# Fused attention and two feed-forward layers on one core: the cosine from one sine with a quarter turn, six of eight unit pairs by seven block products, and two parts of a product in plain float32

## The chip, the cores and the metric

The kernel runs on one core of one Trainium2 chip. The time is the device time of one execution in microseconds (us); the kernel before took 519.95 us as the median of three runs. Everything below about the kernel before comes from one profiled execution of it.

## The reference, cut to what matters

```python
# q, k, v: (2, 12, 448, 64); x: (896, 768); w_in: (768, 2048); w_out: (2048, 768)
scores = cap * tanh(q @ k.T / 8 / cap)
x = softmax(scores) @ v            # heads side by side: 896 tokens x 768
h = x @ moe_w_in
x = (h * cos(h)) @ moe_w_out       # first feed-forward layer
h = x @ moe2_w_in
out = (h / (1 + exp(-h))) @ moe2_w_out
```

Everything is float32 in and out. TensorE multiplies here mostly in the format float32r: a float32 number is split into a high part, rounded to float32r, and a low part, the rest, and a product of two matrices is made of three matmuls (high by high, high by low, low by high). A matmul in plain float32 needs no split and no third product, but it goes over the moving matrix more than once: the trace lists it as two matmul instructions.

## The kernel before, in words

The attention (lines 167 to 413) goes through 12 pairs of heads in an order written out by hand. Everything after it is planned: the functions `gemm_in`, `gemm_out`, `gemm_sums` and `gemm_last` only make a list of tasks, each with an engine, a cost in ns, the values that it reads and writes, and a due time; `run_plan` (L512) then goes through that list in a simulated time, gives each engine that is free the ready task with the earliest deadline for which buffers are left, and issues the instructions in the order so found. The order on each engine is thus fixed when the kernel is built. Deadlines are worked back from TensorE's tasks (`pe`, L485), which are due at the sum of the costs of the matmuls ahead of them. The costs of the others are the linear formulas in `act` (L471, ScalarE), `dve` (L474, VectorE) and `dma` (L466).

The four matrix products are these. All of them are cut in two by two blocks, and most are done with seven block products in place of eight (Winograd's form of Strassen's method), for which sums of blocks must be formed first and sums of results afterwards.

- `gemm_in` (L896), first layer's input product. The 2048 columns are handled as 8 pairs `p` of two blocks of 128 columns. For the first `PLAIN` = 3 pairs (L99) every block is multiplied as it stands (`one_side`, `half_prods`): 2 blocks by 2 halves of the tokens by 6 slices by 3 float32r matmuls, 72 of them. For the others (`m1` to `m7`, `ORDER1` at L615) there are seven block products of 9 matmuls (`block_prod`, L884), 63 of them. A plain pair needs two weight blocks, each brought to float32 (`convert`, L649: two instructions on ScalarE, one on VectorE, the join at L663) and split (`split`, L669: the high part is a copy on ScalarE, L625, the low part a subtraction on VectorE, L628 or, negated, L631). A pair by seven products needs the same two conversions, four sums of half blocks (`ADDS`, `sums`), which the list `S1E` puts on VectorE or on accumulating DMAs of the POOL queue, the splits of the four weight operands (`A`, `S31`, `S24`, and `A22` of half the size), three copies out of PSUM on ScalarE (`m1`, `m5_`, `m6`) and two additions on VectorE (`m7`, `m3`).
- `unit` (L933) makes h cos(h) from a finished 128x448 block of h in PSUM, 32 times. It writes round(h / 2 pi) as an integer (ScalarE, L938), subtracts it from h / 2 pi (VectorE, L939), takes the sine of pi times that (ScalarE, L941), squares it (ScalarE, L942) and multiplies (sine squared - 1/2) by h (VectorE, L943), which is -1/2 h cos(h).
- `gemm_out` (L755), first layer's output product: seven products (`product`, L729) of 4 parts `q`. A part is three PSUM banks by 6 float32r matmuls, after a split of its weights (`split_w`, 768 columns) and of its activations (`split_g`, 896 columns). The tuple `WHOLE` (L622) names the parts done in plain float32 without a split: parts 0, 1 and 2 of the first product, each three banks by 2 matmuls. Split activations lie in tiles of the stock `dbl`: five, of which two are given to the raw weights (L1210, L1212), so at most three groups of activations are split ahead. Sums of activations are made by `sum_g` (list `GE`), sums of weights by `w_sum` (list `WE`), on VectorE or by accumulating DMAs.
- `gemm_sums` (L1029): second layer's input product, all 8 pairs by seven products; `S3E` places the sums of half blocks, `silu` (L1041) applies the activation.
- `gemm_last` (L1121): second layer's output product, seven products of four parts. Its 16 weight blocks are converted beforehand, by the due times in `DUE` (L605), stored to DRAM and fetched again; `LE` places the sums of weights.

The matmuls of all four stages are issued at one line, L684 (`mms`). VectorE's two-operand instructions are mostly at L628 (`sub_`), ScalarE's copies at L625 (`copy`).

Of the kernel before, what the change touches and what calls it, by code (L numbers as in the profile page):

```python
# [28 lines left out]
F32 = mybir.dt.float32  # L29
F32R = mybir.dt.float32r  # L30
I32 = mybir.dt.int32
U32 = mybir.dt.uint32
U8 = mybir.dt.uint8
AF = mybir.ActivationFunctionType
ALU = mybir.AluOpType
# [3 lines left out]
def tile_attention_ffn_ffn(  # L39
# [10 lines left out]
    nc = tc.nc  # L50
    B, H, S, D = shape
    DM = out.shape[0]
    DFF = w_in1.shape[0] * 128
    P = 128
# [15 lines left out]

    capt = const.tile([P, 1], F32, name="capt")
    scap = const.tile([P, 1], F32, name="scap")

    def get_scap(cap):
        nc.vector.tensor_copy(capt, cap)
# [20 lines left out]
    xt = [[Part(f"x{j}_{b}") for b in range(B)] for j in range(KD)]  # L96

    KMAX = KD
    PLAIN = 3  # L99
    FIRST_IN = [b * HP + n for n in range(HP) for b in range(2)]  # L100
    wjobs = []
    for w_in, w_out in ((w_in1, w_out1), (w_in2, w_out2)):
# [66 lines left out]
    with ExitStack() as actx:  # L169
# [19 lines left out]
        def v_init():  # L189
            nc.gpsimd.memset(ones[:, :2 * Q], 1.0)  # L190
            nc.gpsimd.memset(ones[:, 2 * Q:], 0.0)

# [243 lines left out]
            self.after, self.next, self.vals = set(), [], []  # L438

    tasks = []  # L440
    LAT = {"X": 0, "PE": 280, "SP": 3500, "POOL": 400, "ACT": 210, "DVE": 170}
    stock = {"ring": room, "bank": [], "half": halves, "dbl": doubles, "one": [], "raw": []}

    def do(eng, cost, fn, r=(), w=(), due=1e9, moves=0, lag=0, extra=()):
# [18 lines left out]
        tasks.append(t)  # L463
        return t

    def dma(eng, kb, fn, r, w, adds=False, **k):  # L466
        rate = 0.16 if adds else 0.38 if kb > 450 else 0.24
        cost = 350 if eng == "SP" else 900 if adds else 600
        do(eng, cost, fn, r, w, moves=kb * 1.024 / rate, lag=1700 if eng == "POOL" else 600, **k)

    def act(n, fn, r, w, **k):  # L471
        do("ACT", 1.03 * (14 + 0.963 * n), fn, r, w, **k)

    def dve(n, fn, r, w, one=False, **k):  # L474
        do("DVE", 1.03 * (95 + (0.521 if one else 1.0417) * n), fn, r, w, **k)

    def plus(eng, kb, o, a, b, r, w):
        if eng == "DMA":
# [33 lines left out]
    def run_plan(free_at):  # L512
        from heapq import heappop, heappush
        for t in tasks:
            for p in t.after:
                p.next.append(t)
        for t in reversed(tasks):
            t.dl = min([t.due] + [s.dl - t.cost - t.lat for s in t.next])
        vals = list({id(v): v for t in tasks for v in t.vals if v.pool}.values())
        queue = {k: [] for k in stock}  # L520
        for v in vals:
            v.dl = min((t.dl, t.n) for t in v.tasks)
            v.left = len(v.tasks)
            if not v.held:
                queue[v.pool].append(v)
        for q in queue.values():
            q.sort(key=lambda v: v.dl)
        count = {k: len(s) for k, s in stock.items()}
        ready = {e: [] for e in LAT}
        busy = {e: free_at.get(e, 0) for e in LAT}  # L530
        events = [(0, -1, None)] + [(x, -1, None) for x in busy.values()]
        started, line = [], 0
        for t in tasks:
            t.wait = len(t.after)
            if t.eng == "X":
                t.start = 0
                started.append(t)
                events.append((t.cost, t.n, t))
            elif not t.wait:
                ready[t.eng].append(t)  # L540
        events.sort()
        while events:
            now = events[0][0]
            while events and events[0][0] == now:
                _, _, t = heappop(events)
                if t is None:
                    continue
                for s in t.next:
                    s.wait -= 1
                    if not s.wait:  # L550
                        ready[s.eng].append(s)
                for v in t.vals:
                    if v.pool:
                        v.left -= 1
                        if not v.left:
                            for k, n in (v.gives[1] if v.gives else [(v.pool, v.n)]):
                                count[k] += n
            for e in LAT:
                if busy[e] > now:
                    continue  # L560
                for t in sorted(ready[e], key=lambda t: (t.dl, t.n)):
                    want = [v for v in t.vals if not v.held]
                    ok = True
                    for k in {v.pool for v in want}:
                        last = max(queue[k].index(v) for v in want if v.pool == k)
                        ok = ok and sum(v.n for v in queue[k][:last + 1]) <= count[k]
                    if not ok:
                        continue
                    for v in want:
                        v.held = True  # L570
                        queue[v.pool].remove(v)
                        count[v.pool] -= v.n
                    ready[t.eng].remove(t)
                    t.start = now
                    started.append(t)
                    busy[e] = now + t.cost
                    heappush(events, (busy[e], -1, None))
                    end = busy[e] + t.lat
                    if t.moves:
                        line = max(busy[e] + 1000, line) + t.moves  # L580
                        end = line + 1000 + t.lag
                    heappush(events, (end, t.n, t))
                    break
        if len(started) < len(tasks):
            stuck = sorted((t for t in tasks if not hasattr(t, "start")), key=lambda t: t.dl)[:8]
            raise RuntimeError([(t.eng, t.dl, t.wait, t.fn.__name__, [(v.pool, v.held, v in queue.get(v.pool, ()) and queue[v.pool].index(v)) for v in t.vals]) for t in stuck] + [count])
        for v in vals:
            v.left = len(v.tasks)
        for t in sorted(started, key=lambda t: (t.start, t.n)):
            for v in t.vals:  # L590
                if v.pool and v.buf is None:
                    take_buf(v)
            if t.fn:
                t.fn()
            for v in t.vals:
                if v.pool:
                    v.left -= 1
                    if not v.left:
                        give_buf(v)

    NORMS = 6900, 9700
    GE, WE, LE = [["DVE", "DMA"][n] for n in (0, 0, 0, 1)], [["DVE", "DMA"][n] for n in (0, 0, 1, 0)], [["DVE", "DMA"][n] for n in (0, 1)]
    FE = "DVE"
    S3E = [["DVE", "DMA"][n] for n in (1, 1, 0, 0, 0, 0, 0, 0)]
    DUE = [220000, 234000, 248000, 262000, 276000, 290000, 304000, 318000, 332000, 346000, 360000, 374000, 1000000000, 1000000000, 1000000000, 1000000000]  # L605
    base_s = KF + 4 * (HK + 1)
    base_l = base_s + KF

    S1E = [["DVE", "DMA"][n] for n in (1, 0, 1, 0, 1, 1, 0, 0)]
    HALF1 = [('half', 'ring'), ('half', 'half'), ('half', 'half'), ('ring', 'ring'), ('half', 'ring'), ('half', 'ring'), ('half', 'half'), ('ring', 'ring')]  # L610
    low, high = range(KD - 2), range(KD - 2, KD)
    PLAIN_ORDER = [(0, 0), (1, 0), (2, 0), (0, 1, low), (1, 1, low), (0, 1, high), (1, 1, high), (2, 1)]
    for n in range(3, 2 * PLAIN):
# [5 lines left out]
    ORDER1.append((4, HP - 1))  # L619


    WHOLE = ((0, 1, 2), (), (), (), ())  # L622

    def copy(out, src, scale=1.0):
        nc.scalar.activation(out=out, in_=src, func=AF.Copy, scale=scale)  # L625
# [23 lines left out]
    def convert(i, out, outs, view, due=1e9, pool="raw"):  # L649
# [12 lines left out]
        def f_join():  # L662
            nc.vector.scalar_tensor_tensor(out=view(), in0=w(1), scalar=3, in1=w(0), op0=ALU.logical_shift_left, op1=ALU.bitwise_or)  # L663
        k = {"due": due}
        act(n, f_word, [], [raw], **k)
        act(n, f_scale, [], [raw], **k)
        dve(n, f_join, [raw], outs, **k)

    def split(n, hi, lo, vhi, vlo, src, r, neg=False):  # L669
        act(n, lambda: copy(vhi(), src(), -1.0 if neg else 1.0), r, [hi])  # L670
        dve(n, lambda: (neg_sub if neg else sub_)(vlo(), src(), vhi().bitcast(F32)), [hi, *r], [lo])

    def pair_of(pool="half"):
# [222 lines left out]
    def gemm_in():  # L896
# [36 lines left out]
        def unit(name, p, bank):  # L933
            t, subs = y_in(name, p // 2, gx)
            c = p % 2
            h, r = lambda: bank.buf[:, :S], lambda: t.buf[:, c, :]
            w = [subs[c]]
            act(S, lambda: copy(r().bitcast(I32), h(), 1.0 / (2.0 * math.pi)), [bank], w)  # L938
            dve(S, lambda: nc.vector.scalar_tensor_tensor(out=r(), in0=h(), scalar=1.0 / (2.0 * math.pi), in1=r().bitcast(I32),  # L939
                                                          op0=ALU.mult, op1=ALU.subtract), [bank], w)  # L940
            act(S, lambda: nc.scalar.activation(out=r(), in_=r(), func=AF.Sin, scale=math.pi), [table], w)  # L941
            act(S, lambda: nc.scalar.activation(out=r(), in_=r(), func=AF.Square), [], w)  # L942
            dve(S, lambda: nc.vector.scalar_tensor_tensor(out=r(), in0=r(), scalar=-0.5, in1=h(), op0=ALU.add, op1=ALU.mult), [bank], w, due=clock["pe"] + 5000)  # L943

        both_m = {}

# [319 lines left out]
```

## Time and profile before

| | |
|---|---|
| median of 3 runs | 519.95 us (519.59 to 520.43) |
| profiled execution | 519.64 us, of it 517.8 us from the first to the last instruction |
| TensorE busy | 99% |
| VectorE busy | 82% |
| ScalarE busy | 80% |
| granted TensorE clock | 1.000 |

Times in the profile are from the span's start. A line of a group of instructions names the source line, the engine (PE is TensorE, PEld its weight load, DVE is VectorE, ACT is ScalarE, POOL is GpSimd), the operation, what is written and read, the shapes and the number of instructions; then the busy time in us and the mean of one in ns, and the engine's idle time just before them, with the engine that ended it. The tiles are named by role: `bank` is PSUM, `v` a buffer of the planner, `hl` a tile of split weights, `x` the split attention output, `wraw` weights as loaded, `e`, `sc` and `scap` belong to the attention.

### The profile page before, as it was taken

Reading aid. Unit: us, or ns where it says so; the run is one execution under the profiler, and the core shown is the slowest. Engines: PE = TensorE matmul, PEld = TensorE weight load, DVE = VectorE, ACT = ScalarE, POOL = GpSimd, SP = SyncE. Lnnn points to the kernel's source line nnn. Section 1 sums busy time; section 2 is a strip of 40 time slices with the busy share of each in tenths; the row PEclk is TensorE's granted clock in tenths of the full one; section 3 lists DMA queues with packets and bytes.
Section 4 is the critical chain, followed back from the end, with each engine's and each line's share of the span. In section 5 each row is a group of like instructions: output and inputs, shape, how many; then the busy total and the mean of one; then the engine's idle time right before and its main releaser. Section 6 shows DMA issues by size and latency. Waiting matters only on the chain.

```text
span 517.8 us, 7246 instructions
## 1 busy us (share of the span) xinstructions
PE 510.7 (99%) x2637; PEld 420.4 (81%) x2637; DVE 424.8 (82%) x597; ACT 413.3 (80%) x583; POOL 63.3 (12%) x86
## 2 busy tenths in 40 slices
PE   8999999999999999999999999999999999999997
PEld 5444443799999997699999999999999999999996
DVE  5388997999989899999999999876779878965660
ACT  6999998699999989999777594999989664546341
POOL 0145442000210000001401111000000011400000
PEclk9999999999999999999999999999999999999999
DMA  8146464288615135799973343978798975940111
GB/s 308 59 128 192 123 206 135 78 332 238 170 31 184 61 108 197 240 330 273 196 200 84 88 104 80 375 268 299 282 346 275 381 140 105 246 92 0 54 53 54
DMA packets 27559, 92.12 MB, mean 178 GB/s; under 512 B 4536, under 2 KB 10212, under 8 KB 27524
## 3 DMA queue, kind: packets, MB, share of 16 engines
q1 hardware_dynamic: 19488, 70.89, 39.6%
q0 software_dynamic: 7680, 20.45, 18.1%
q8 instruction: 21, 0.34, 0.3%
q10 hardware_dynamic: 356, 0.32, 0.2%
q14 instruction: 14, 0.11, 0.1%
HBM read 72.75 MB, written 10.66 MB: 161 GB/s over the span
## 4 chain that ended last, share of the span: by engine, by line
PE 96%; ACT 2%; issue 1%; DVE 0%
PE bank L684 81%; PE po L273 5%; PE sc L239 4%; PE sm L291 2%; PE sc L243 2%; PE po L283 2%; ACT e L251 1%; PE warm L347 1%; ACT e L257 1%; DVE e L299 0%; DVE zero L356 0%; DVE v L1204 0%; ACT v L625 0%; PE sm L284 0%; DVE sums L318 0%
## 5 line engine op out<-in xcount | busy, mean ns | idle before, releaser
L684 PE MATMUL bank<-v,hl 128*128 128x448 f32 x1449 | 301.5, 367 | 0.0
L684 PEld LDWEIGHTS bank<-v,hl 128*128 128x128 f32 x1449 | 272.1, 188 | 25.5 <-issue 0.7
L628 DVE TENSOR_TENSOR v<-v,v 128x896 fp32r<-128x896 f32 (+4 forms) x112 | 108.7, 991 | 30.7 <-ACT v L625 30.1
L625 ACT ACTIVATE v<-v 128x896 fp32r<-128x896 f32 (+2 forms) x83 | 70.0, 853 | 56.4 <-PE bank L684 49.6
L628 DVE TENSOR_TENSOR hl<-v,hl 128x768 fp32r<-128x768 f32 (+1 forms) x89 | 79.2, 898 | 5.2 <-ACT hl L625 4.9
L625 ACT ACTIVATE hl<-v 128x768 fp32r<-128x768 f32 (+1 forms) x89 | 70.0, 797 | 1.3 <-PE bank L684 1.1
L684 PE MATMUL bank<-x,hl 128*128 128x448 f32 x288 | 59.9, 366 | 0.0
L625 ACT ACTIVATE v<-bank 128x448 f32<-128x448 f32 (+2 forms) x82 | 43.8, 541 | 18.8 <-PE bank L684 17.9
L684 PEld LDWEIGHTS bank<-x,hl 128*128 128x128 f32 x288 | 54.0, 188 | 5.0 <-DVE xs L310 0.7
L657 ACT ACTIVATE wraw<-wraw 128x768 int32<-128x768 uint8 x61 | 55.3, 917 | 2.9 <-DMA wraw<-in_moe_w_out 2.8
L660 ACT ACTIVATE wraw<-wraw 128x768 f32<-128x768 f32 x61 | 55.5, 913 | 0.0
L684 PE MATMUL bank<-v,v 128*128 128x448 f32 x225 | 54.8, 395 | 0.0
L684 PEld LDWEIGHTS bank<-v,v 128*128 128x128 f32 x225 | 42.3, 188 | 9.3 <-issue 5.9
L251 ACT ACTIVATE e<-sc,scap 128x896 f32<-128x896 f32 (+1 forms) x48 | 40.0, 911 | 6.7 <-PE sc L239 6.7
L479 POOL DMA_DIRECT2D v<-v x24 | 22.5, 936 | 167.2 <-ACT v L625 95.3
L663 DVE SCALAR_TENSOR_TENSOR v<-wraw 128x768 int32<-128x768 int32 x40 | 37.9, 952 | 5.7 <-ACT wraw L660 5.1
L257 ACT ACTIVATE e<-e,capt 128x3136 f32<-128x3136 f32 (+2 forms) x13 | 35.2, 2709 | 0.4
L273 PE MATMUL po<-e,vf 128*64 128x448 f32 x144 | 29.4, 540 | 0.4 <-ACT e L257 0.4
L273 PEld LDWEIGHTS po<-e,vf 128*64 128x64 f32 x144 | 10.2, 137 | 17.3 <-issue 16.3
L312 POOL DMA_DIRECT2D sums<-xs x22 | 17.5, 801 | 49.8 <-DVE sums L318 41.1
L628 DVE TENSOR_TENSOR v<-v 128x384 f32<-128x384 f32 (+1 forms) x42 | 23.2, 561 | 0.3
L1143 POOL DMA_DIRECT2D v<-wd x8 | 7.0, 878 | 126.6 <-DVE hl L628 102.1
(77 smaller groups left out, 460.8 us busy)
## 6 DMA issues: line engine op xcount, KB each, us to landing
wraw<-in_moe_w_out SPq DMA_DIRECT2D x32, 768.0 KB, 5.5
wraw<-in_moe_w_in SPq DMA_DIRECT2D x29, 768.0 KB, 6.6
wd<-wx SPq DMA_DIRECT2D x16, 384.0 KB, 5.4
v<-wd SPq DMA_DIRECT2D x16, 384.0 KB, 7.7
raw<-in_qkv POOLq DMA_DIRECT2D x9, 480.0 KB, 4.7
v<-v POOLq DMA_DIRECT2D x8, 384.0 KB, 7.5
v<-wd POOLq DMA_DIRECT2D x8, 384.0 KB, 6.4
rb<-rs SPq DMA_DIRECT2D x24, 112.0 KB, 3.5
```

What stands on the lines that cost most here:

```text
L239: nc.tensor.matmul(ps[:, u, :S], kk[rows, cols], qq[rows, :S], start=m == 0, stop=m == 2)
L251: nc.scalar.activation(out=e32[p][:, 2 * t:2 * t + n, :], in_=sc.pop((p, t))[:, :n, :S], func=AF.Tanh, scale=scap)
L257: nc.scalar.activation(out=e, in_=e, func=AF.Exp, scale=capt)
L273: nc.tensor.matmul(po[u * D:(u + 1) * D], vf[p][:, 2 * t + u, :], e32[p][:, 2 * t + u, :], start=first and n == 0, stop=last and n == len( ...
L312: (nc.gpsimd if p < NPT - 1 else nc.scalar).dma_start(sums[p][:, y], x[y * Q:y * Q + D + 1:D])
L479: dma("POOL", kb, lambda: nc.gpsimd.dma_start(o(), b(), accum_op=ALU.add), r, w, adds=True)
L625: nc.scalar.activation(out=out, in_=src, func=AF.Copy, scale=scale)
L628: nc.vector.tensor_tensor(out=out, in0=a, in1=b, op=op)
L657: nc.scalar.activation(out=b[:, :, 0], in_=b.bitcast(U8)[:, :, 3], func=AF.Copy, scale=1.0 / 32, bias=-0.5 + 1.0 / 64)
L660: nc.scalar.activation(out=w(1).bitcast(F32), in_=w(1).bitcast(F32), func=AF.Prelu, scale=2.0 ** -112, alpha=2.0 ** 32)
L663: nc.vector.scalar_tensor_tensor(out=view(), in0=w(1), scalar=3, in1=w(0), op0=ALU.logical_shift_left, op1=ALU.bitwise_or)
L684: nc.tensor.matmul(bank, x, y, start=first and m == 0, stop=last and m == len(ops) - 1, skip_group_check=True)
```

## The change

- `unit`: the integer is round(h / 2 pi + 1/4), the sine is taken of 2 pi times the difference plus a quarter turn, which is cos(h), and the square is left out. The quarter turn, pi / 2, is the bias of the sine instruction, read from a one-column tile `quarter` that GpSimd fills at the start. The last multiplication has the factor -1/2. The number of VectorE instructions stays.
- `PLAIN` goes from 3 to 2: pair 2 is done by seven block products. `S1E` has the sums of pair 2 on DMAs and those of pairs 3 to 7 on VectorE; before, pairs 4 and 5 had theirs on DMAs, pairs 3, 6 and 7 on VectorE.
- `WHOLE`: part 1 of the first product of `gemm_out` is split and done in float32r like the others; parts 0 and 2 stay in plain float32.
- The planner: the cost formulas of ScalarE and VectorE have other constants, with a margin of 1% where there were 3%. The high part of a split of under 800 columns becomes a task of a new kind, `COPY`: ScalarE may take it as any other, and VectorE takes it where ScalarE's queue of tasks with earlier deadlines would end less than 1000 ns ahead of the copy's deadline, or later.
- Placement: of the sums of weights in `gemm_out`, the last set is on DMAs in place of the third; in `gemm_last` both sets are on DMAs, where the first was on VectorE; in `gemm_sums` the sums of pair 2 are on DMAs. The due times of the conversions for `gemm_last` are 10 us apart in place of 14. `HALF1` exchanges the places of two pairs' split weights.

```diff
--- before.py
+++ after.py
@@ -70,6 +70,7 @@
     scap = const.tile([P, 1], F32, name="scap")
+    quarter = const.tile([P, 1], F32, name="quarter")
@@ -96,7 +97,7 @@
     KMAX = KD
-    PLAIN = 3
+    PLAIN = 2
     FIRST_IN = [b * HP + n for n in range(HP) for b in range(2)]
@@ -189,6 +190,7 @@
             nc.gpsimd.memset(ones[:, 2 * Q:], 0.0)
+            nc.gpsimd.memset(quarter, math.pi / 2.0)
@@ -438,7 +440,7 @@
     tasks = []
-    LAT = {"X": 0, "PE": 280, "SP": 3500, "POOL": 400, "ACT": 210, "DVE": 170}
+    LAT = {"X": 0, "COPY": 210, "PE": 280, "SP": 3500, "POOL": 400, "ACT": 210, "DVE": 170}
     stock = {"ring": room, "bank": [], "half": halves, "dbl": doubles, "one": [], "raw": []}
@@ -463,16 +465,19 @@
+    SPARE = 1000
+    MARGIN = 1.01
+
...
     def act(n, fn, r, w, **k):
-        do("ACT", 1.03 * (14 + 0.963 * n), fn, r, w, **k)
+        do("ACT", MARGIN * (90 + 0.84 * n), fn, r, w, **k)
     def dve(n, fn, r, w, one=False, **k):
-        do("DVE", 1.03 * (95 + (0.521 if one else 1.0417) * n), fn, r, w, **k)
+        do("DVE", MARGIN * (66 + 1.05 * n), fn, r, w, **k)
@@ -556,9 +561,12 @@
             for e in LAT:
-                if busy[e] > now:
+                if busy[e] > now or e == "COPY":
                     continue
-                for t in sorted(ready[e], key=lambda t: (t.dl, t.n)):
+                free = ready["COPY"] if e == "ACT" else []
+                if e == "DVE":
+                    free = [t for t in ready["COPY"] if max(now, busy["ACT"]) + sum(x.cost for x in ready["ACT"] + ready["COPY"] if x.dl < t.dl) > t.dl - SPARE]
+                for t in sorted(ready[e] + free, key=lambda t: (t.dl, t.n)):
                     want = [v for v in t.vals if not v.held]
@@ -571,6 +579,9 @@
                     ready[t.eng].remove(t)
+                    if t.eng == "COPY":
+                        t.eng, t.lat = e, LAT[e]
+                        t.cost = t.other if e == "DVE" else t.cost
                     t.start = now
@@ -599,15 +610,15 @@
     NORMS = 6900, 9700
-    GE, WE, LE = [["DVE", "DMA"][n] for n in (0, 0, 0, 1)], [["DVE", "DMA"][n] for n in (0, 0, 1, 0)], [["DVE", "DMA"][n] for n in (0, 1)]
+    GE, WE, LE = [["DVE", "DMA"][n] for n in (0, 0, 0, 1)], [["DVE", "DMA"][n] for n in (0, 0, 0, 1)], [["DVE", "DMA"][n] for n in (1, 1)]
     FE = "DVE"
-    S3E = [["DVE", "DMA"][n] for n in (1, 1, 0, 0, 0, 0, 0, 0)]
-    DUE = [220000, 234000, 248000, 262000, 276000, 290000, 304000, 318000, 332000, 346000, 360000, 374000, 1000000000, 1000000000, 1000000000, 1000000000]
+    S3E = [["DVE", "DMA"][n] for n in (1, 1, 1, 0, 0, 0, 0, 0)]
+    DUE = [220000, 230000, 240000, 250000, 260000, 270000, 280000, 290000, 300000, 310000, 320000, 330000, 1000000000, 1000000000, 1000000000, 1000000000]
     base_s = KF + 4 * (HK + 1)
...
-    S1E = [["DVE", "DMA"][n] for n in (1, 0, 1, 0, 1, 1, 0, 0)]
-    HALF1 = [('half', 'ring'), ('half', 'half'), ('half', 'half'), ('ring', 'ring'), ('half', 'ring'), ('half', 'ring'), ('half', 'half'), ('ring', 'ring')]
+    S1E = [["DVE", "DMA"][n] for n in (1, 0, 1, 0, 0, 0, 0, 0)]
+    HALF1 = [('half', 'ring'), ('half', 'half'), ('half', 'half'), ('half', 'ring'), ('ring', 'ring'), ('half', 'ring'), ('half', 'half'), ('ring', 'ring')]
     low, high = range(KD - 2), range(KD - 2, KD)
@@ -619,7 +630,7 @@
-    WHOLE = ((0, 1, 2), (), (), (), ())
+    WHOLE = ((0, 2), (), (), (), ())
@@ -662,12 +673,23 @@
         k = {"due": due}
-        act(n, f_word, [], [raw], **k)
-        act(n, f_scale, [], [raw], **k)
+        do("ACT", MARGIN * 800, f_word, [], [raw], **k)
+        do("ACT", MARGIN * 800, f_scale, [], [raw], **k)
         dve(n, f_join, [raw], outs, **k)
...
     def split(n, hi, lo, vhi, vlo, src, r, neg=False):
-        act(n, lambda: copy(vhi(), src(), -1.0 if neg else 1.0), r, [hi])
+        if n < 800:
+            def go():
+                if t.eng == "ACT":
+                    copy(vhi(), src(), -1.0 if neg else 1.0)
+                elif neg:
+                    nc.vector.tensor_scalar(out=vhi(), in0=src(), scalar1=-1.0, scalar2=None, op0=ALU.mult)
+                else:
+                    nc.vector.tensor_copy(vhi(), src())
+            t = do("COPY", MARGIN * (90 + 0.84 * n), go, r, [hi])
+            t.other = 100 + 0.5 * n
+        else:
+            act(n, lambda: copy(vhi(), src(), -1.0 if neg else 1.0), r, [hi])
         dve(n, lambda: (neg_sub if neg else sub_)(vlo(), src(), vhi().bitcast(F32)), [hi, *r], [lo])
@@ -935,12 +957,11 @@
             w = [subs[c]]
-            act(S, lambda: copy(r().bitcast(I32), h(), 1.0 / (2.0 * math.pi)), [bank], w)
+            act(S, lambda: nc.scalar.activation(out=r().bitcast(I32), in_=h(), func=AF.Copy, scale=1.0 / (2.0 * math.pi), bias=0.25), [bank], w)
             dve(S, lambda: nc.vector.scalar_tensor_tensor(out=r(), in0=h(), scalar=1.0 / (2.0 * math.pi), in1=r().bitcast(I32),
                                                           op0=ALU.mult, op1=ALU.subtract), [bank], w)
-            act(S, lambda: nc.scalar.activation(out=r(), in_=r(), func=AF.Sin, scale=math.pi), [table], w)
-            act(S, lambda: nc.scalar.activation(out=r(), in_=r(), func=AF.Square), [], w)
-            dve(S, lambda: nc.vector.scalar_tensor_tensor(out=r(), in0=r(), scalar=-0.5, in1=h(), op0=ALU.add, op1=ALU.mult), [bank], w, due=clock["pe"] + 5000)
+            act(S, lambda: nc.scalar.activation(out=r(), in_=r(), func=AF.Sin, scale=2.0 * math.pi, bias=quarter), [table], w)
+            dve(S, lambda: nc.vector.scalar_tensor_tensor(out=r(), in0=r(), scalar=-0.5, in1=h(), op0=ALU.mult, op1=ALU.mult), [bank], w, due=clock["pe"] + 5000)
```

## Rows read from the trace of the kernel before

**Rows 1.** Busy time, share, instructions of each engine, and the costliest group (the page).
```profile
PE 510.7 (99%) x2637; PEld 420.4 (81%) x2637; DVE 424.8 (82%) x597; ACT 413.3 (80%) x583; POOL 63.3 (12%) x86
...
L684 PE MATMUL bank<-v,hl 128*128 128x448 f32 x1449 | 301.5, 367 | 0.0
```

**Rows 2.** Chain of work that ended last, in order of time: start, length, what.
```profile
93.59 420.63 PE bank L684 x2025
...
514.63 0.39 DVE v L1204
```

**Rows 3.** Timeline of TensorE, three stretches: start, length, what, number of instructions.
```profile
99.70 4.62 PE L684 MATMUL bank<-x,hl 128*128 128x448 f32 x22
...
204.57 10.69 PE L684 MATMUL bank<-v,v 128*128 128x448 f32 x28
...
439.64 4.71 PE L684 MATMUL bank<-v,hl 128*128 128x448 f32 x22
```

**Rows 4.** Stretches: length, busy PE, PEld, DVE, ACT, POOL; granted clock, DMA share, GB/s.
```profile
91.00:123.00 32.00, 32.00 (x161) 28.12 (x158) 29.90 (x52) 27.12 (x44) 1.85 (x2) 1.00 0.65 219
123.00:160.00 37.00, 37.00 (x184) 34.27 (x183) 34.19 (x56) 36.19 (x67) 5.17 (x6) 1.00 0.53 136
160.00:200.00 40.00, 40.00 (x197) 36.72 (x196) 36.40 (x59) 37.15 (x69) 0.00 (x0) 1.00 0.36 132
200.00:218.00 18.00, 18.00 (x60) 11.05 (x59) 16.50 (x22) 17.98 (x29) 0.00 (x0) 1.00 0.54 169
218.00:260.00 42.00, 42.00 (x209) 38.93 (x208) 40.31 (x43) 38.27 (x51) 6.99 (x8) 1.00 0.96 275
260.00:310.00 50.00, 50.00 (x249) 46.34 (x248) 48.14 (x65) 37.95 (x58) 5.22 (x6) 1.00 0.48 117
...
310.00:410.00 100.00, 100.00 (x488) 91.27 (x487) 82.39 (x116) 88.79 (x138) 1.74 (x2) 1.00 0.81 285
410.00:514.00 104.00, 104.00 (x505) 94.31 (x503) 69.01 (x74) 48.80 (x65) 10.63 (x12) 1.00 0.42 101
```

**Rows 5.** Groups of instructions of ScalarE by line and shape.
```profile
L625 ACT ACTIVATE hl<-v 128x768 fp32r<-128x768 f32 x77 | 64.4, 841 | 0.2 <-DVE v L628 0.2
...
L625 ACT ACTIVATE v<-v 128x896 fp32r<-128x896 f32 x53 | 50.5, 953 | 53.5 <-PE bank L684 49.6 <-issue 3.3 <-DVE v L628 0.5
...
L625 ACT ACTIVATE v<-bank 128x448 f32<-128x448 f32 x46 | 24.9, 541 | 15.8 <-PE bank L684 15.5
L942 ACT ACTIVATE v<-v 128x448 f32<-128x448 f32 x32 | 18.3, 582 | 0.1
L941 ACT ACTIVATE v<-v 128x448 f32<-128x448 f32 x32 | 18.2, 583 | 0.8 <-DVE v L939 0.8
...
L251 ACT ACTIVATE e<-sc,scap 128x448 f32<-128x448 f32 x12 | 7.7, 639 | 0.0
```

**Rows 6.** Groups of instructions of VectorE by line and shape.
```profile
L628 DVE TENSOR_TENSOR hl<-v,hl 128x768 fp32r<-128x768 f32 x77 | 73.0, 952 | 5.0 <-ACT hl L625 4.7
L628 DVE TENSOR_TENSOR v<-v,v 128x896 fp32r<-128x896 f32 x41 | 44.7, 1090 | 26.7 <-ACT v L625 26.2
...
L628 DVE TENSOR_TENSOR v<-v 128x384 f32<-128x384 f32 x36 | 19.9, 552 | 0.3
...
L628 DVE TENSOR_TENSOR v<-bank,v 128x448 f32<-128x448 f32 x28 | 16.9, 619 | 3.1 <-PE bank L684 2.9
...
L339 DVE CAST x<-xv 128x448 fp32r<-128x448 f32 x12 | 4.7, 395 | 0.4
```

**Rows 7.** Timeline of VectorE from 218 us: neighbours, and one split.
```profile
218.91 2.09 DVE L628 TENSOR_TENSOR v<-v,v 128x896 f32<-128x896 f32 x2
...
223.76 1.09 DVE L631 SCALAR_TENSOR_TENSOR v<-v,v 128x896 fp32r<-128x896 f32 x1
```

**Rows 8.** DMA issues by what they move: number, KB each, us to landing.
```profile
v<-v POOLq DMA_DIRECT2D x8, 384.0 KB, 7.5
...
v<-v POOLq DMA_DIRECT2D x12, 192.0 KB, 3.1
```

## The prediction

> **What bounds the kernel now.** I read the page's busy times first: TensorE is busy 99% of the span [rows 1]. Busy matmuls overlap, so that alone says little; the chain of waits, in order of time, says more. From 93.59 us on it is one piece, 420.63 us of matmuls of L684, 2025 instructions, and after it only the copies and stores of the last block follow [rows 2]. In the groups these matmuls have an idle time of 0.0 [rows 1]. So after the attention the time is the number of matmuls times their pitch, and no other engine is waited for.
>
> The pitch comes from TensorE's timeline. A matmul of mean length 0.367 us [rows 1] is followed by the next after some 0.20, so the last of a stretch sticks out by 0.16. The stretch at 99.70 gives (4.62 - 0.16) / 22 = 0.2027 us, the one at 439.64 (4.71 - 0.16) / 22 = 0.2068, the plain float32 stretch at 204.57 (10.69 - 0.16) / 28 = 0.376 [rows 3]. The kernel has 3 x 72 + 5 x 63 = 531 float32r matmuls in the first input product, 25 x 18 = 450 in the first output product, 504 in each of the last two stages: 1989. The 18 plain ones appear as 36 records; 1989 + 36 are the 2025 of the chain. Check: (420.63 - 36 x 0.376) / 1989 = 0.2047, between the two pitches.
>
> Then I read the stretches, for how near the other engines are to being waited for [rows 4]. VectorE's idle time is 2.10, 2.81, 3.60, 1.50, 1.69 and 1.86 us in the six stretches from 91 to 310 us, 13.6 us in all, 11.7 of it by 260; then 17.6 and 35.0 in the last two. ScalarE has 24.3 us up to 310, 4.9 of it in the first one. The clock is granted in full (1.00, the 2.4 GHz level) in all of them.
>
> **The change on TensorE, which sets the end.** Pair 2 goes from 72 matmuls to 63: 9 x 0.2027 = 1.82 us less. The part that leaves plain float32 gives up 6 matmuls of 2 x 0.376, 4.51 us, and takes 18 of 0.2027, 3.65: 0.86 us less. Sum: 2.7 us less, with 2022 records in the chain. Nothing else in the diff adds or removes a matmul, and these counts are fixed by the code: that they don't fall is no rival.
>
> **ScalarE, off the path.** The square goes: 32 x 0.582 = 18.6 us less at most [rows 5]; the next instruction starts before the last one ends, so some 0.47 each, 15 us. The sine's bias is now a column of memory. No row shows that for a sine; the nearest is the 448-column tanh of the attention, which reads its scale from a column: 0.639 against 0.541 for a copy of the same shape out of PSUM [rows 5]. Between 0 and 0.1 us each, 0 to 3.1 in all; I take 3.1, since it is the same kind of operand. The Trainium skill, "ScalarE: Activation LUTs", section "What ACT_TABLE_LOAD costs", says that each one-column operand adds about 93 ns; by it this would be 3.0 us, and the tanh row agrees. The integer's added 1/4 is a constant in the instruction: 0, bounded by the same 0.1. Pair 2 adds three 768-column copies and a half one for two, and three copies of 0.541: 0.841 + 0.5 (half of the columns: between half of 0.841 and 0.541) + 1.6 = 3 us. The new split adds 0.841 + 0.953 = 1.8. ScalarE so loses some 7 us up to 220 us, and this covers every cost just named; without that cover, each would delay VectorE's subtraction that follows it.
>
> **VectorE, the close one.** Pair 2: three 768-column subtractions and a half one in place of two, two additions: 0.952 + 0.552 + 2 x 0.619 = 2.7 us. Sums of half blocks: 12 before, 20 after, 8 x 0.552 = 4.4. The new split: 0.952 + 1.090 = 2.0 [rows 6]. In all 9.2, or 8.2 us where neighbours overlap: two of 1.084 take 2.09 [rows 7], so 0.08 comes off for each of 13. Sums of weights in the first output product: still 12 on VectorE, but the third set, 4 x 0.87 = 3.5, falls ahead of about 260 us, where it was on DMAs. Up to 310 us VectorE must fit 8.2 us more into 2.7 us less, out of 13.6 us of idle time: 2.7 us remain. By 260 us it needs 8.2 + 3.5 + 2.7 = 14.4 out of 11.7: 2.7 us too much, unless work done ahead of need is put off. There is such work. The last of the four negated splits of the second product starts at 223.76 and ends at 224.85 [rows 7]; TensorE reaches its group after the plain stretch (to 215.1) and four groups of 18 x 0.2027, at 229.7. That is 4.9 us ahead. With three tiles for split activations it can be 11 us ahead at most. So I cost VectorE at nothing on the path: 4.9 us of lead covers 2.7 of lateness, and ScalarE's lighter load takes away some of the idle time that VectorE spends waiting for copies (26.2 us in one group over the whole kernel [rows 6], though most of it late). Copies that the planner hands to VectorE cost it 0.395 each for 448 columns [rows 6]; they are taken only where ScalarE is behind, and from 91 to 220 us it has just been relieved.
>
> **DMAs and order.** Pair 2 by seven products starts 14.6 us earlier (72 x 0.2027), after two plain pairs, 29.2 us into the stage, and its operands T1 to T4 too. Its four sums are DMAs of 192 KB, 3.1 us to landing [rows 8], for eight before in the stage, four after. In `gemm_last` a set of four 384 KB sums moves from VectorE (0.95 each) to DMAs: 0.9 us to issue on POOL as that queue's others (10.63 us for 12 [rows 4]), 7.5 to landing [rows 8], 8.4 in all, behind up to three of its own kind in the queue. A weight part is free after its split for one product and needed for the next 4 x 18 x 0.2068 = 14.9 us later; so some 6 us spare, less the splits' lead. Cost 0, bounds 0 to 3. Conversions for `gemm_last` fall 4 us each earlier, up to 44; ScalarE has 11.2 us idle from 310 to 410 [rows 4] and up to four more conversions there, of two instructions of some 0.84 each, take 7: it fits, and the short copies may go to VectorE, which has 17.6. The memset on GpSimd is ahead of the first real matmul: 0.
>
> **Sum.** The profiled execution took 519.64 us, 1.84 more than its span; 519.64 - 2.7 = 516.9. The median stands 0.31 higher: 517.3 us.
>
> **Rivals.**
> - *VectorE is the bound from about 200 to 260 us.* For it: 2.7 us remain of 13.6 in my sum, each instruction waits for something now and then, and the planner's margin falls from 3% to 1%. Against: lead, and the relief of ScalarE. It decides from the point where half of the idle time cannot be filled: then by 260 us VectorE is 2.7 + 5.9 = 8.6 us late, less 4.9 of lead, 3.7 us of waiting on TensorE, and the time is 521.0, slower than before.
> - *The pitch changes.* The two pitches of rows 3 differ by 4 ns with nothing in the code to say why; a stage of 504 matmuls that goes over is 2.0 us. The last stage at 0.2027: 515.3. A stage now at 0.2027 going to 0.2068: 519.2. Against: most of the order on TensorE stays.
> - *A sum by DMA is late*, for pair 2 or in `gemm_last`: one landing of 3.1, at 520.4. For it: the bounds above. Against: transfers have shares to spare (0.65 and 0.42 busy in these stretches [rows 4]). The Trainium skill, "SBUF — State Buffer", section "SBUF: two separate sides", holds that a copy from float32 on VectorE locks GpSimd out while it writes descriptors for such a DMA; by it each copy handed to VectorE could add its 0.4 us to a sum beside it. No row here shows a POOL issue so prolonged; with 6 us spare it would take many at once, and by rows it ends at 520.4 as well: 0.01 of this rival's chance.
>
> **How the numbers follow.** TensorE stays fed: 0.66, 516.6 to 518.0. VectorE bound: 0.14, 518.9 to 522. Pitch faster 0.06, slower 0.08. DMA late 0.06. A measurement of this kernel can tell about 0.2%, 1.0 us, from no change. Under 518.9 lie the first case, the fast pitch and a little of the rest: 0.75; within 1.0 us the slow pitch, the late DMA and mild cases of VectorE: 0.14; above 521.0 the rest of VectorE's: 0.11. The range of 515.3 to 520.4 leaves out part of VectorE's case and little of the fast pitch.
>
> **What would show it.** Right: one unbroken piece of L684 with 2022 records from 93.6 us to 511.5, no waits of PE or PEld on DVE or ACT of over 0.3 us, no group at L942, VectorE over 97% busy from 91 to 310 us, the sine about 0.1 us longer, ScalarE's idle time up to 310 us above 30. Wrong: idle time of L684 put down to DVE around 200 to 260 us, or a pitch away from 0.2027 ahead of 310 us, or from 0.2068 after 410, or waits on DMAs behind the sums at L479.

## The result, and the profile after

The changed kernel took 514.29 us in the median of 4 runs (513.87 to 514.91), the kernel before 519.86 beside it: ratio 0.9891, 95% interval 0.9873 to 0.9908. It is faster, as forecast, but by 5.6 us in place of 2.6, and 1.0 us below the low end of the range.

The page's busy times, and the chain of work that ended last (start, length, what), of the changed kernel; they answer to [rows 1, 2]:

```profile
PE 504.6 (99%) x2634; PEld 419.1 (82%) x2634; DVE 425.9 (83%) x608; ACT 404.3 (79%) x553; POOL 66.5 (13%) x91
```

```profile
93.25 415.11 PE bank L706 x2022
...
508.77 0.39 DVE v L1225
```

The matmuls are still one unbroken piece, with the 2022 records that the count gave. But it is 5.52 us shorter, where 9 + 6 x 2 records fewer and 18 more were worth 2.7. The rest is in the pitch. TensorE's timeline in the stretches of [rows 3]:

```profile
99.77 4.42 PE L706 MATMUL bank<-x,hl 128*128 128x448 f32 x21
...
207.51 4.67 PE L706 MATMUL bank<-v,v 128*128 128x448 f32 x12
...
439.67 4.62 PE L706 MATMUL bank<-v,hl 128*128 128x448 f32 x22
```

With the tail of 0.16 taken off, the first is 0.2027 us a matmul as before, the plain float32 one 0.376 as before, and the last stage (4.62 - 0.16) / 22 = 0.2027, where it was 0.2068: 504 x 4.0 ns = 2.0 us. The stage ahead of it changed too, in part: in the changed kernel its matmuls go over between the two pitches every few dozen. The busy times of the two late stages' matmuls (length, PE, PEld, then granted clock, DMA share, GB/s), of before and then of after:

```profile
310.00:405.00 95.00, 95.00 (x464) 86.68 (x463) 1.00 0.80 279
412.00:505.00 93.00, 93.00 (x452) 84.47 (x451) 1.00 0.44 102
```

```profile
310.00:405.00 95.00, 95.00 (x467) 87.35 (x466) 1.00 0.87 300
412.00:505.00 93.00, 93.00 (x461) 86.18 (x460) 1.00 0.43 97
```

A stretch counts the matmuls cut at its two ends, so two come off: 95 / 462 = 0.2056 and 95 / 465 = 0.2043, 93 / 450 = 0.2067 and 93 / 459 = 0.2026. The granted clock is 1.00 in all four. So of the span's 5.9 us, 2.7 are the count, 2.8 the pitch (5.52 - 2.68), and 0.34 the start of the piece, which in the profiles of kernels with this same attention lies anywhere from 93.1 to 93.8.

The other engines, in stretches as in [rows 4]:

```profile
91.00:123.00 32.00, 32.00 (x159) 28.23 (x156) 30.02 (x55) 26.04 (x41) 1.86 (x2) 1.00 0.61 183
123.00:160.00 37.00, 37.00 (x183) 34.04 (x182) 36.96 (x63) 34.64 (x60) 1.72 (x2) 1.00 0.45 139
160.00:200.00 40.00, 40.00 (x195) 36.41 (x195) 39.70 (x65) 35.27 (x58) 0.00 (x0) 1.00 0.42 138
200.00:218.00 18.00, 18.00 (x74) 13.52 (x73) 17.84 (x23) 17.97 (x27) 0.00 (x0) 1.00 0.65 235
218.00:260.00 42.00, 42.00 (x209) 38.93 (x208) 41.74 (x46) 36.72 (x50) 6.94 (x8) 1.00 0.95 270
260.00:308.00 48.00, 48.00 (x239) 44.45 (x238) 46.57 (x64) 36.51 (x55) 6.08 (x7) 1.00 0.51 138
```

VectorE's idle time up to 308 us is 1.98 + 0.04 + 0.30 + 0.16 + 0.26 + 1.43 = 4.2 us, 2.7 by 260; it was 13.6 and 11.7. From 91 us on TensorE's weight loads wait on it twice, 0.7 us for `xs` at the end of the attention and 0.2 us behind it (what ended the idle time, us in all, times, longest; `issue` is time in which nothing that the profile shows was waited for):

```profile
PEld bank L706 <- issue: 4.5, 24, 0.2
PEld po L275 <- issue: 0.9, 4, 0.2
PEld bank L706 <- DVE xs L312: 0.7, 1, 0.7
PEld bank L706 <- DVE v L639: 0.2, 1, 0.2
```

The sine, and the copies that the planner gave to VectorE:

```profile
L963 ACT ACTIVATE v<-v,quarter 128x448 f32<-128x448 f32 x32 | 21.0, 670 | 1.5 <-DVE v L961 1.5
```

```profile
L688 DVE CAST hl<-v 128x768 fp32r<-128x768 f32 x3 | 1.7, 555 | 0.0
L688 DVE CAST v<-v 128x768 fp32r<-128x768 f32 x1 | 0.6, 552 | 0.0
...
L688 DVE CAST v<-v 128x448 fp32r<-128x448 f32 x1 | 0.4, 384 | 0.0
```

The sine takes 0.087 us more than the old one's 0.583 [rows 5]. The Trainium skill, "ScalarE: Activation LUTs", section "What ACT_TABLE_LOAD costs", gives some 93 ns for a one-column operand; the trace agrees, with 87. Five copies in all went to VectorE.

### The profile page after: what moved, and what is told of

Read it like the earlier page. It is cut to its first block, busy times and chain, and to the rows that moved or that the text cites. A ratio compares the mean times of both kernels' runs of the same rounds, so it can differ in the third digit from the quotient of the medians.

```text
span 511.9 us, 7243 instructions
## 1 busy us (share of the span) xinstructions
PE 504.6 (99%) x2634; PEld 419.1 (82%) x2634; DVE 425.9 (83%) x608; ACT 404.3 (79%) x553; POOL 66.5 (13%) x91
## 4 chain that ended last, share of the span: by engine, by line
PE 96%; ACT 2%; issue 1%; DVE 0%
PE bank L706 81%; PE po L275 5%; PE sc L241 4%; PE sm L293 2%; PE sc L245 2%; PE po L285 2%; ACT e L253 1%; PE warm L349 1%; ACT e L259 1%; DVE e L301 0%; DVE zero L358 0%; DVE v L1225 0%; ACT v L636 0%; PE sm L286 0%; DVE sums L320 0%
## 5 line engine op out<-in xcount | busy, mean ns | idle before, releaser
L706 PE MATMUL bank<-v,hl 128*128 128x448 f32 x1494 | 308.7, 366 | 0.0
L706 PEld LDWEIGHTS bank<-v,hl 128*128 128x128 f32 x1494 | 280.5, 188 | 23.9 <-issue 1.1
L639 DVE TENSOR_TENSOR hl<-v,hl 128x768 fp32r<-128x768 f32 (+1 forms) x92 | 81.7, 894 | 3.1 <-ACT hl L636 3.0
L484 POOL DMA_DIRECT2D v<-v x28 | 26.2, 964 | 205.0 <-ACT wraw L671 108.1
L706 PE MATMUL bank<-v,v 128*128 128x448 f32 x222 | 51.9, 384 | 0.0
L706 PE MATMUL bank<-x,hl 128*128 128x448 f32 x216 | 45.5, 366 | 0.0
L706 PEld LDWEIGHTS bank<-x,hl 128*128 128x128 f32 x216 | 40.5, 188 | 4.0 <-DVE xs L312 0.7
L674 DVE SCALAR_TENSOR_TENSOR v<-wraw 128x768 int32<-128x768 int32 x42 | 39.6, 951 | 2.5 <-ACT wraw L671 2.4
L636 ACT ACTIVATE v<-bank 128x448 f32<-128x448 f32 (+2 forms) x52 | 27.6, 534 | 13.9 <-PE bank L706 13.8
L639 DVE TENSOR_TENSOR v<-v 128x384 f32<-128x384 f32 (+1 forms) x46 | 25.5, 559 | 0.2
L639 DVE TENSOR_TENSOR v<-bank,v 128x448 f32<-128x448 f32 x28 | 16.9, 619 | 9.1 <-PE bank L706 8.9
```

Source lines behind the costliest of these rows:

```text
L484: dma("POOL", kb, lambda: nc.gpsimd.dma_start(o(), b(), accum_op=ALU.add), r, w, adds=True)
L639: nc.vector.tensor_tensor(out=out, in0=a, in1=b, op=op)
L706: nc.tensor.matmul(bank, x, y, start=first and m == 0, stop=last and m == len(ops) - 1, skip_group_check=True)
```

## The experiments

Ratios are to the kernel before on the same chip, with their 95% intervals. "Piece" is the row of matmuls that the chain shows, and pitches are read as above.

**The count.** Two kernels undo one part of TensorE's saving each.

```diff
-    PLAIN = 2
+    PLAIN = 3
```

> The changed kernel with three plain pairs as before, all else as changed. By the count: 9 matmuls more, 1.8 us more, 516.1, with 2031 records in the chain. If the pitch is a state picked up by chance, up to 2 us either way beside that, read from the stages' pitches; the count's term is then the difference that is left after the pitches.

515.69 us, 0.9918 (0.9905 to 0.9932). The piece:

```profile
93.32 417.23 PE bank L706 x2031
```

It is 2.1 us longer than the changed kernel's, of it 0.2 a wait at 243 us and the rest the 1.8 of the count within 0.1.

```diff
-    WHOLE = ((0, 2), (), (), (), ())
+    WHOLE = ((0, 1, 2), (), (), (), ())
```

> The changed kernel with parts 0, 1 and 2 of the first product in plain float32 as before, all else as changed. By the count: 6 matmuls of 0.752 for 18 of 0.2027, 0.86 us more, 515.2, with 2016 records in the chain. A pitch picked up by chance may add or take up to 2 us, to be read from the stages' pitches.

514.57 us, 0.9898 (0.9883 to 0.9913):

```profile
93.25 415.90 PE bank L706 x2016
```

That is 0.8 us longer, against 0.86 by the count. The medians, 0.3 apart, can't tell these two kernels from each other; the profiles do. Both terms of the sum stand, and both kernels have the short pitch in the last stage: neither part brought it.

**What the pitch hangs on.** One short matmul ahead of the first of `gemm_last`, in the kernel before (`ones` is a float32 tile of the attention):

```diff
+    def reset(bank):
+        nc.tensor.matmul(bank.buf[:32, :32], ones[:, :32], ones[:, :32], start=True, stop=True)
...
                 def go(q=q, k=k, whi_=whi_, wlo_=wlo_, v=v, flat=flat):
+                    if d is gf and fresh and key == "A" and q == 0 and k == 0:
+                        reset(banks[k])
                     ops = []
```

> The kernel before, with one matmul of 32x32 in plain float32 put ahead of the very first matmul of gemm_last; the order of everything else is the same. Theory (state): the pitch of 0.2027 or 0.2067 us is a state that TensorE carries on from matmul to matmul; plain float32 matmuls leave it in the short one, as after the plain stretch at 215 us. Then the last stage goes over to 0.2027: 504 x 4 ns, 2.0 us less, 517.9. Rival (place): the pitch comes from where operands lie and what runs beside in that stage. Then nothing changes but the added matmul, under 0.2 us: 519.9 to 520.1, pitch 0.2067 after 410 us.

518.17 us, 0.9965 (0.9952 to 0.9977). Its timeline in the last stage:

```profile
439.81 4.42 PE L687 MATMUL bank<-v,hl 128*128 128x448 f32 x21
```

That is 0.2029, the short pitch, where the kernel before has 0.2068 with the same matmuls in the same order. Operands, places and order are those of before; one matmul ahead of them decides. So the pitch is a state that runs on from matmul to matmul. Is the plain format needed?

```diff
-                        reset(banks[k])
+                        few = flat(whi_)[:, :32]
+                        nc.tensor.matmul(banks[k].buf[:32, :32], few, few, start=True, stop=True)
```

> As the first experiment, the kernel before with one 32x32 matmul ahead of the first of gemm_last, but this one in float32r, the format of its neighbours. If it is the plain format (a passage over the moving matrix of another kind) that puts TensorE in the short pitch: 0.2067 stays after 410 us, 519.8 to 520.0. If any short matmul that breaks the row does it: 0.2027 after 410 us, 2.0 us less, 517.9.

517.64 us, 0.9958 (0.9944 to 0.9972), and the short pitch in the last stage again:

```profile
439.65 4.62 PE L684 MATMUL bank<-v,hl 128*128 128x448 f32 x22
```

A short float32r matmul does it as well: the format is not needed. Up to the added matmul the two kernels, the plain one first, also show how well the pitches repeat where the places are the same:

```profile
93.75 316.45 PE bank L687 x1521
93.25 316.46 PE bank L684 x1521
```

Whole executions repeat less well: those of the second kernel lie at 517.4 to 517.6 or at 518.4 to 518.8 us, and only one of the first group was profiled.

What sends TensorE into the long pitch? An unused tile ahead of all others leaves the order as it is and moves the operands:

```diff
+    const.tile([P, 16], F32, name="pad")
     capt = const.tile([P, 1], F32, name="capt")
```

> The kernel before with an unused tile of 64 bytes per partition ahead of all others: same instructions in the same order, operands 64 bytes further on. If the order of TensorE's instructions decides when the pitch goes over: the same sequence, long from 181 us and from 410 us, 519.9. If the places of the operands decide: another sequence, with 504 matmuls of the last stage at 0.2027 or others longer, 516 to 523.

> As before with 448 bytes in place of 64. If the order decides: again the same sequence as in the kernel before, 519.9. If the places decide at a coarser grain than 64 bytes, this one differs where the other did not.

One execution each: 516.60 us with 64 bytes, 519.96 with 448. Their pieces, 64 bytes and then 448:

```profile
93.60 417.59 PE bank L685 x2025
```

```profile
93.25 421.32 PE bank L685 x2025
```

The work is that of [rows 2], 2025 records in 420.63 us, and every engine runs the same instructions in the same order. The kernel before never took less than 519.17 us beside any of the experiments, so 516.60 lies well outside its spread. So the places of the operands decide where the pitch goes over; whether it is TensorE's own operands or those of the engines beside it is not separated, for the tile moves them all. With 448 bytes the time is the old one, but the sequence is not: the pitch is long from 155 us on in the first product, where it was from 183, and the piece is 0.7 us longer. The change has a new tile of its own, `quarter`, ahead of `ones` and all that follows:

```diff
     scap = const.tile([P, 1], F32, name="scap")
+    const.tile([P, 1], F32, name="quarter")
```

> The kernel before with the tile of the quarter turn allocated and never used: same order, operands moved by that one column. If the places that the change happens to give its operands are behind the shorter pitch: the last stage at 0.2027 and the one ahead of it at 0.203 to 0.204, 517 to 517.5. If the new order is behind it: the pitches of before, 519.9.

518.80 us, 0.9974 (0.9962 to 0.9985): between the two. Its late stages:

```profile
310.00:405.00 95.00, 95.00 (x467) 87.37 (x466) 1.00 0.81 281
412.00:505.00 93.00, 93.00 (x452) 84.47 (x451) 1.00 0.43 100
```

The tile alone gives the shorter pitch of the stage from 310 us (467, as after), not that of the last one. Taken out of the changed kernel:

```diff
-    quarter = const.tile([P, 1], F32, name="quarter")
...
-            nc.gpsimd.memset(quarter, math.pi / 2.0)
...
         recip(NPT - 1)
+        quarter = ones[:, :1]
+        nc.gpsimd.memset(quarter, math.pi / 2.0)
```

> The changed kernel with the quarter turn kept in a column of the tile of ones, which the attention no longer needs by then: same work, same order, operands where they would be without the new tile. If the tile's shift is behind the shorter pitch: long pitch in the last stage, 516 to 517. If not: 514.3, pitches as in the changed kernel.

514.88 us, 0.9901 (0.9875 to 0.9926): the late stages stay at 467 and 461, while the first product gets longer (piece 415.94). So the tile is not what keeps the changed kernel's late stages short. What does is open: the changed kernel and all ten variants of it here have the last stage in the short pitch, whichever part of the work they undo, and none of them undoes the planner, `LE` or `DUE`. The new cosine alone, in the kernel before:

> The kernel before with the new cosine alone: no matmul fewer, 32 instructions of ScalarE fewer. Theory: TensorE was waited for by all and waits for nobody, so the time is that of before, 519.9, but for the pitch, which a new order may change by up to 2 us in each late stage, down to 517. Rival: ScalarE's load was felt somewhere: waits or idle time of TensorE that go away; there are none in the trace of before, so this would be below 519.9 at the same pitches.

518.99 us, 0.9983 (0.9974 to 0.9992), 2025 records in 420.06 us, no wait of over 0.3 us behind the attention, the long pitch in the last stage. The cosine removes nothing that TensorE waited for.

**What keeps TensorE fed.** The old `unit` in the changed kernel:

```diff
-            act(S, lambda: nc.scalar.activation(out=r(), in_=r(), func=AF.Sin, scale=2.0 * math.pi, bias=quarter), [table], w)
+            act(S, lambda: nc.scalar.activation(out=r(), in_=r(), func=AF.Sin, scale=math.pi), [table], w)
+            act(S, lambda: nc.scalar.activation(out=r(), in_=r(), func=AF.Square), [], w)
...
```

> The changed kernel with the old cosine (sine of half the angle, squared): 32 squares more on ScalarE, TensorE's matmuls those of the changed kernel. Theory A: the cosine only made room on ScalarE, and the copies that may go to VectorE do not replace that: waits of TensorE appear between 94 and 310 us, 1 to 5 us in all, 515 to 519. Rival B: the new planner alone keeps TensorE fed: 514.3 within 0.7 us of pitch. The number of matmul records in the chain stays 2022 in both.

517.32 us, 0.9949 (0.9934 to 0.9964). TensorE's weight loads wait on VectorE, at 133 and 239 us:

```profile
PEld bank L706 <- DVE hl L639: 2.6, 2, 1.4
```

That is some 2.4 us of 3.0; after the second wait the first output product runs in the long pitch. VectorE is busy all of the time from 123 to 160 us (37.00 of 37.00), and 13 copies went to it in place of 5. So without the 15 us that the new cosine frees on ScalarE, TensorE waits; how much of that is load and how much the new order that the planner makes of it is not separated. One plain part fewer (`WHOLE = ((0,), ...)`), and none:

> The changed kernel with only part 0 of the first product in plain float32. By the count, 0.86 us less, 513.4, with 2028 records. VectorE gets 2.0 us more by 215 us, where its idle time from 123 to 260 us is 0.8 us in the changed kernel. Theory A (VectorE's lead of a few us covers it): 513.4. Rival B (VectorE is at its limit): TensorE waits up to 2 us on VectorE between 200 and 260 us, 514 to 516.

> The changed kernel with no part in plain float32. By the count, 1.7 us less, 512.6, with 2034 records. VectorE gets 4 us more, TensorE 1.7 less, against 0.8 us of idle time from 123 to 260 us. Theory A (lead covers it): 512.6. Rival B (VectorE at its limit): waits of 2 to 5 us on VectorE, 514.5 to 517.5; also, without a plain stretch the pitch of the first output product may be the long one, up to 2.0 us more.

515.82 us, 0.9926 (0.9908 to 0.9943), and 518.86, 0.9974 (0.9962 to 0.9987). With one part, the stretch where it happens, and the waits:

```profile
218.00:260.00 42.00, 40.47 (x196) 36.21 (x195) 42.00 (x47) 35.72 (x47) 6.97 (x8) 1.00 0.95 275
```

```profile
PEld bank L706 <- DVE hl L639: 2.4, 3, 1.4
```

VectorE has no idle time left there, TensorE 1.5 us: the rival of the prediction, one step beyond the change. Without any plain part the time is above the rival's 514.5 to 517.5, though the first output product keeps the short pitch: the waits are 2.5 us on VectorE's `hl` and 3.0 on ScalarE, and from 230 to 240 us the granted clock is 0.83. Two plain pairs in the kernel before, then the same with the new `S1E`:

```diff
-    PLAIN = 3
+    PLAIN = 2
```

```diff
-    S1E = [["DVE", "DMA"][n] for n in (1, 0, 1, 0, 1, 1, 0, 0)]
+    S1E = [["DVE", "DMA"][n] for n in (1, 0, 1, 0, 0, 0, 0, 0)]
```

> The kernel before with two plain pairs in place of three and nothing else. By the count 1.8 us less, 518.1. Theory (ScalarE and VectorE have no room without the cosine and the new planner): TensorE waits 1 to 5 us between 94 and 310 us, 519 to 523. Rival (counts decide): 518.1, or down to 515.5 if the last stages fall into the short pitch.

> The kernel before with two plain pairs and the new S1E, old cosine and old planner. If S1E alone made the variant with two plain pairs slow: 518.1 by the count, or less with a shorter pitch. If ScalarE's load with the squares counts as well: waits of 1 to 4 us remain, 519 to 522.

525.60 us, 1.0113 (1.0093 to 1.0133), and 517.10, 0.9947 (0.9930 to 0.9964). The list alone is worth 8.5 us; of them some 2 us are the pitch of the last stage, long in the first and short in the second (389 and 397 matmuls from 425 to 505 us). The rest is mostly waits: 3.7 us on VectorE and 3.9 on ScalarE in the first, 1.1 and 1.4 in the second. In the changed kernel, `S1E` undone:

> The changed kernel with the sums of pairs 4 and 5 on DMAs as before (S1E undone, all else as changed). VectorE has 3.8 us less. If it is the load of VectorE that decides: 514.3, no waits, idle time of VectorE up by 4 us. If the placement on DMAs, whose longer latency moves the planner's deadlines and so the order from the second pair on, is what made the three slow variants wait at 124, 136 and 176 us: the same waits here, 518 to 523.

525.10 us, 1.0104 (1.0079 to 1.0129). The stretch where it loses most:

```profile
123.00:160.00 37.00, 33.63 (x156) 29.98 (x155) 31.62 (x53) 28.31 (x49) 5.20 (x6) 0.95 0.47 117
```

TensorE is idle for 3.4 us there, but VectorE for 5.4 and ScalarE for 8.7: this is no load, but an order. A part of the loss is the clock. TensorE stood idle for 1.91 us, and soon after it the granted clock fell to 0.50, the 1.2 GHz level, for some 3 us, in which nine matmuls took 0.373 us each, 1.5 us more than at 0.203:

```profile
126.84 2.52 PE L706 MATMUL bank<-x,v 128*128 128x448 f32 x9 [1.91 <-ACT bank L636]
```

```profile
128.50:131.50 3.00, 3.00 (x10) 0.50 0.75 115
```

The order on VectorE departs from the changed kernel's ahead of the sums of pair 2: the joins of weights (L674) come at 112.43 and 114.45 us, where the changed kernel has the next one at 116.47, and six accumulating DMAs start by 131.2 us, where it has the four of pair 2. So work for a later pair now comes ahead of work for pair 2. That the planner's deadlines do it, which count a DMA's long way against the tasks ahead of it, is read from `run_plan` (L518) and not shown. Nor is it separated from the loads: those of weights issued at 113.45 and 115.44 us took 7.2 us each, where the changed kernel's next one, at 117.50, took 5.0. Three tries for a faster version, with part of VectorE's sums given back to DMAs, fell to the same: `S1E` undone with one plain part or none, and with the third set of `WE` on DMAs too.

> The changed kernel with only part 0 in plain float32, and with the sums of pairs 4 and 5 given back to DMAs (8 x 0.47 = 3.8 us off VectorE for the 2.0 that the split adds). If VectorE's load alone made the variant with one plain part slower: no waits, 2028 records, 0.9 us less than the changed kernel, 513.4. If the place of the work counts (the burst of splits ahead of 240 us) rather than its sum: waits of about 1 us remain, 514.5 to 515.5.

> The same with no part in plain float32: VectorE has 4.0 us more and 3.8 less than in the changed kernel, with 1.7 us less of TensorE's time to hide in. If the sum of VectorE's work decides: waits of at most 1.7 us, 512.6 to 514.3. If the burst of splits and conversions ahead of 240 us decides: 515 to 518, as without the DMAs.

> As the variant with one plain part and pairs 4 and 5 on DMAs, and the third set of sums of weights in the first output product on DMAs too (3.5 us off VectorE ahead of 260 us). If VectorE decides: 513.4, no waits. If the accumulating DMAs, 8 in that stretch in place of 4, come late: waits on DMAs at the sums, 514 to 517.

522.64, 526.47 and 524.45 us (1.0052, 1.0133 and 1.0082, each interval above 1), all above the times expected. None beats the changed kernel.

## Why the prediction was wrong

- **The term that was mis-sized is the pitch.** The sum kept the pitches of [rows 3] in each stage and so put their change at nothing, because "most of the order on TensorE stays"; the rival in which the last stage falls to 0.2027 had a chance of 0.06 and stood alone, without the stage before it. Measured: 2.0 us in the last stage, 0.8 in the others, beside the count's 2.7. A pitch away from 0.2068 after 410 us was among its signs of being wrong, and it came. The order was the wrong thing to look at: with the order unchanged, 64 bytes took 3.0 us off the piece. A re-planned kernel hands out its buffers anew, so each stage's pitch was open; the last stage, long throughout before, could only gain, and the one ahead of it mostly. That it gained, and not lost, was luck as far as the forecast goes: which part of the change did it is open.
- **The count was right**: 2022 records, 1.8 and 0.86 us, each shown by undoing it.
- **VectorE at nothing on the path was right, and close.** Its idle time up to about 310 us came to 4.2 us for the 2.7 of the sum; one wait of 0.2 us. By 260 us, where the sum had 2.7 us too much work, 2.7 us were left: VectorE had done 9.0 us more there than before, not 8.2 + 3.5. Whether the rest was put off, as the lead allowed, or sized too high was not read. The rival's point lies one plain part further on.
- **ScalarE's relief as the cover was right in direction**: without it, 3.0 us are lost. Its idle time up to 310 us, 29.9 us, just missed the sign of over 30.
- **The sums moved to VectorE were read wrongly.** The prediction counted them as 4.4 us of load and nothing else. Undone, they free VectorE and cost 10.8 us, through waits and the clock after them, not through VectorE's load. None of the rivals had this.
- **DMAs**: no wait on a sum shows in the changed kernel's weight loads; cost 0, as taken.

## What to carry to other kernels

Where TensorE never waits, read its pitch stage by stage, and hold a difference of a few ns that no code explains for a term of its own: here it was half of the gain and could have come without the change. Undo a change's placements one at a time before crediting its arithmetic; two flags of a list were worth more than the matmuls saved. With VectorE 98% busy, the next matmuls saved were paid back at once.

## What the runs showed of the hardware

- Matmuls of 128x128 weights by 448 float32r columns, in an unbroken row, run at 0.2027 or 0.2067 us for long stretches, at a granted clock of 1.00: the whole last stage of 504 is at one or the other. In the stage ahead of it both occur, with means of 0.2043 and 0.2056. One 32x32 matmul in the row brought the short one back for the 504 that followed, at a cost of some 0.1 us in its trace in float32r and 0.4 in plain float32 (517.64 and 518.17 us, against 519.70 and 519.79).
- Which one holds depends on the places of the operands: 64 bytes further on, the same instructions took 417.59 us for 420.63 (one execution). The Trainium skill, "SBUF — State Buffer", section "SBUF: two separate sides", knows of contention among engines only at the port that VectorE and GpSimd share; no run here tells whether the 4 ns come from another engine or from TensorE alone. Which places are bad, and why, stays open; only two shifts and one column were tried, and no shift of the changed kernel beyond its own tile.
- After 1.91 us without a matmul, TensorE's granted clock fell from 1.00 to 0.50 (the 1.2 GHz level) for some 3 us, with matmuls at 0.373 us for 0.203: a wait on the path cost 1.5 us beyond itself.
